# Attention followed by a squared-ReLU MLP: the order in which the MLP visits blocks of tokens and parts of the inner dimension

## The chip, the core and the metric

The kernel runs on one core of a Trainium2 chip. The metric is the time of one execution on the device in microseconds (us), lower is better. Engines go by the profile's names: PE (TensorE), DVE (VectorE), ACT (ScalarE), POOL (GpSimd) and SP (SyncE, which issues the transfers here).

## What is computed

Four batches of 576 tokens go through attention with 8 heads of 64 and a learned position bias; the result, 2304 tokens by 512, goes through an MLP with an inner dimension of 2048. Everything comes and leaves in float32.

```python
def _attn_ref(q, k, v, w1, b1, w2):                 # (4, 8, 576, 64)
    scores = scale * np.matmul(q, k.transpose(0, 1, 3, 2)) + bias(w1, b1, w2)
    attn = softmax(scores)
    return np.matmul(attn, v)

def _moe_ref(x, w_in, w_out):                       # x 2304 x 512, d_ff 2048
    h = x @ w_in
    r = np.maximum(h, 0.0)
    g = r * r
    return g @ w_out
```

## The kernel before

The attention fills the first 373 us and is not touched, but for two small copies that the change adds near its end. The rest, from 373 us to the end, is the MLP, and this text is about it.

**Blocks and parts.** The tokens are cut into five blocks: blocks 0 to 3 are the first 512 tokens of each batch (256 columns wide, since a block is worked on as two halves by a seven-product scheme that saves an eighth of the matmuls), and block 4, `B` in the code and "the tail" in this text, is the 64 last tokens of all four batches, 128 columns wide. The inner dimension is cut into eight parts `P` of 256. One **item** is a block with a part, (n, P); there are 40 of them, and the list `items` gives their order. Items are numbered by their place in that list, from 0.

**One item.** `up(i)` makes 42 matmuls on PE into two PSUM tiles, `ha` (24) and `hb` (18). ACT (line 758) and DVE (lines 760 to 763) put the products together from PSUM; then comes the squared ReLU, on ACT for items below `GA` (lines 765 and 766) and on DVE from there on (line 768). ACT then rounds the result to `gh` (line 773) and DVE takes the remainder `gl` (line 774). `down(i)` makes 24 matmuls (12 for the tail) on four PSUM tiles `y0` to `y3` (two for the tail). The loop emits `up(i)` and then `down(i - 1)`. `ha`, `hb` and each `y` have one buffer, so `up(i + 1)` needs the ACT and DVE readers of item i to be done, and the first `down` of a visit needs the tiles `y` of the visit before it to have been read.

**Visits.** A run of items of one block is a visit. `y` is summed in PSUM over a visit. If a block has another visit to come, its four tiles `y` are copied to tiles `o` and stored to HBM (`py`, line 812). When it comes back, `o` is loaded from there (line 801), DVE adds `y` to it (line 802), and the sum goes out (line 814). Before the change each of the blocks 0 to 3 has two visits of four items, and the tail one of eight, in the middle. The tiles `o` share one ring of two buffers, `stage`, with the loads of raw weights.

**Conversions.** Weights are brought as 64-bit words and are converted on the chip. 24 conversions are left when the MLP starts. `convert(k)` after `up(i)` emits k of them, by the table `WC`; the list `todo` has their order. A conversion of a `w_out` piece is ACT (lines 177 and 243), DVE (lines 180 to 183) and POOL (line 244). One of a `w_in` piece has lines 177 and 180 to 183 too, then POOL (lines 235 to 237), ACT (line 224) and DVE (line 225).

**Splits.** Before the first item of a block its inputs are scaled and split into high and low halves: `split_x`, on POOL (line 626), ACT (line 628) and DVE (line 629), seven pieces (fourteen half-size ones for the tail). It is emitted two items ahead of the block. The scale comes from two one-column matmuls on PE behind an `hb` (line 195). The split inputs of blocks 0 to 3 go to HBM (`store_x`) and are loaded again for the later visit (`load_x`).

A scheduler moves instructions within these rules, so that the order on each engine is not that of the code.

Of the kernel before, what the change touches and what calls it, by code (L numbers as in the profile page):

```python
# [21 lines left out]
B, H, S, D = 4, 8, 576, 64  # L22
# [13 lines left out]
WB, WS, LW, XS, XB, LAG, NE, SC, SN, AH = 40, 3, 4, 48, 70, 1, 13, 22, 16, 2  # L36
WC = (2, 2, 2, 1, 1, 1, 1, 2, 1, 2, 1, 2, 1, 1, 1)
MD, K0, E2, BW, KP, PN, KA = 0x15555, 2, 1, 1, 2, 1, 1
C0, ND, NG, GA, QA, WU, QS = 2, 2, 4, 18, 12, 32, 2
BO, B1 = (3, 5, 8, 10, 13, 15, 18, 20), (12, 3, 8)  # L40
# [9 lines left out]
SC = 41  # L50
SN = 12
AH = 2
WC = (2, 2, 2, 0) + (1,) * 16
ND = 3
NG = 4
GA = 18
KA = 4
QA = 0
WU = 12
# [19 lines left out]
def attention_then_relu2_mlp(ctx: ExitStack, tc: tile.TileContext, q, k, v, cols, w_in, w_out, psi, xmat, dist, out):  # L79
    nc = tc.nc  # L80
    PE, DVE, ACT, POOL, SP = nc.tensor, nc.vector, nc.scalar, nc.gpsimd, nc.sync
# [12 lines left out]
    xT = [keep.tile([128, HP, S], F32, name=f"xT{b}") for b in range(AB)]  # L94
# [67 lines left out]
    def column(w=1):  # L162
        used[0] += w
        return small[:, used[0] - w:used[0]]
# [20 lines left out]
    def largest(src, col):  # L185
        return DVE.tensor_reduce(out=col, in_=src, axis=AX.X if len(src.shape) == 2 else AX.XY, op=ALU.max, apply_absolute_value=True)
# [60 lines left out]
    def is_in(n):  # L247
        return n // 2 % 2 == 0
# [12 lines left out]
    def x_pieces(n):  # L261

        if n < B:
            return [(slice(0, 256), xT[n][:, :, 0:256], xT[n][:, :, 256:512])]
        return [(slice(64 * r, 64 * r + 64), xT[r][:, :, 512:], xT[2 + r][:, :, 512:]) for r in range(2)]

    def x_largest(n):
        cols = column(HP)
        if n < B:
            for c in range(HP):  # L270
                largest(xT[n][:, c, 0:512], cols[:, c:c + 1])
        else:
            for b in range(B):
                largest(xT[b][:, :, 512:], cols[:, b:b + 1])
        return cols


# [269 lines left out]
    todo = [(ic, jb) for ic in chunks for jb in range(0, NJB, 2 if ic == TAIL else 1)]  # L547
# [42 lines left out]
    NB, NP = B + 1, NF // 2  # L590
# [13 lines left out]
    def operand(t):  # L604
        t = t.bitcast(F16).rearrange("p (x c t) -> p x c t", x=2, c=2)
        return t[:, 0], t[:, 1]
# [7 lines left out]
    def split_x(n):  # L614
        sig, w = xsig[n], width[n]
        for m in ORDER:
            hi, lo = (x[:, :, :w] for x in split_to[n % 2][m])
            one, op, two = RIGHT[m]
            if m in XA:
                t = take(0, 9856, 512).rearrange("p (c t) -> p c t", c=2)  # L620
            elif op:
                t = stage_p["p"].tile([128, 2, 256], F32, name="xs", tag="wa", bufs=2)
            for cs, *half in x_pieces(n):
                src = half[one[1]][:, 2 * one[0]:2 * one[0] + 2]
                if op:
                    POOL.tensor_tensor(out=t[:, :, cs], in0=src, in1=half[two[1]][:, 2 * two[0]:2 * two[0] + 2], op=op)
                    src = t[:, :, cs]
                ACT.activation(out=hi[:, :, cs], in_=src, func=AF.Identity, scale=sig)
                DVE.scalar_tensor_tensor(out=lo[:, :, cs], in0=src, scalar=sig, in1=hi[:, :, cs], op0=ALU.mult, op1=ALU.subtract)  # L629
            xs_t[n, m] = (hi, lo)  # L630

    def store_x(n):
        xs_dram[n] = dram.tile([128, 7 * 512], F32, name=f"xs{n}")
        SP.dma_start(out=xs_dram[n], in_=xs_at[n % 2])

    def load_x(n):
        if n % 2 == 0:
            places = [(xs_at[0], range(1, 8))]
        else:
            places = [(xT[2].rearrange("p c s -> p (c s)"), range(1, 5)), (xT[3].rearrange("p c s -> p (c s)"), range(5, 8))]  # L640
        for t, ms in places:
            SP.dma_start(out=t[:, :512 * len(ms)], in_=xs_dram[n][:, 512 * (ms[0] - 1):512 * ms[-1]])
            for k, m in enumerate(ms):
                xs_t[n, m] = operand(t[:, 512 * k:512 * k + 512])
# [8 lines left out]
    for s in range(NU + TL + 1):  # L653
# [32 lines left out]
        if s == XS:  # L686
            pw = ps.tile([128, 512], F32, name="pw", tag="aux", bufs=4)
            set_scale(0, x_largest(0), pw[:, 0:1])
        if s == XB:
            split_x(0)  # L690
        if s < AB * HP * TAIL:
            n, r = divmod(s, AB * HP)
# [7 lines left out]
        if 0 <= s - TL - 1 < NU:  # L700
            values(s - TL - 1)
            b, hp, ic = units[s - TL - 1]
# [17 lines left out]
    ph_p = ctx.enter_context(tc.tile_pool(name="ph", bufs=1, space=PSUM, reuse_waits="tile"))  # L720
    py_p = ctx.enter_context(tc.tile_pool(name="py", bufs=1, space=PSUM, reuse_waits="tile"))

    runs = [(n, 0, NP // 2) for n in range(B)] + [(B, 0, NP)] + [(n, NP // 2, NP) for n in reversed(range(B))]
    items = [(n, P) for n, p0, p1 in runs for P in range(p0, p1)]
    firsts = {(n, p0) for n, p0, p1 in runs}
    lasts = {(n, p1 - 1) for n, p0, p1 in runs}
    part_y = {}
# [3 lines left out]
    def up(i):  # L731
# [31 lines left out]
        stt(out=c[:, 2:4], in0=hb[:, 1:3, :w], scalar=alpha, in1=c[:, 2:4], op0=ALU.mult, op1=ALU.add)  # L763
        if i < GA:
            ACT.activation(out=c, in_=c, func=AF.Relu)
# [58 lines left out]
    def chain_x(n, cols):  # L824
        def run(ps_col):
            set_scale(n, cols, ps_col)
        chains.append(run)


    todo = [4 * P + 2 + f for P in range(NP // 2) for f in range(2)]  # L830
    for P in range(NP // 2, NP, 2):
        todo += sorted(range(4 * P, 4 * P + 8), key=lambda n: (is_in(n) == (P > NP // 2), n))
    done = loaded = 0
    def convert(k):
        nonlocal done, loaded
        for _ in range(k):
            while loaded < min(len(todo), done + AH):
                load_w(todo[loaded])
                loaded += 1
            if done < len(todo):  # L840
                n = todo[done]
                (split_in if is_in(n) else split_out)(n, wdst[n])
                done += 1
# [4 lines left out]
    for i in range(len(items) + LAG):  # L848
        if i == NP // 2:
            tmp_stack.close()  # L850
            late = ctx.enter_context(tc.tile_pool(name="late", bufs=1, side="right", reuse_waits="tile"))
            for n in (4 * NP - 2, 4 * NP - 1):
                t = late.tile([128, 2, 512], F32R, name=f"w{n}")
                wdst[n] = (t[:, 0], t[:, 1])
        if i < len(items):
            n, P = items[i]
            up(i)
            if i + 2 < len(items) and items[i + 2] in firsts and items[i + 2][1] == 0:
                split_x(items[i + 2][0])
            if P == 0 and n < B:  # L860
                store_x(n)
            if P == NP // 2 and n:
                load_x(n - 1)
            if i + 4 < len(items) and items[i + 4] in firsts and items[i + 4][0] not in alpha_t:
                xcols = x_largest(items[i + 4][0])
            if i + 3 < len(items) and items[i + 3] in firsts and items[i + 3][0] not in alpha_t:
                chain_x(items[i + 3][0], xcols)
        convert(WC[i] if i < len(WC) else 0)
        if i >= LAG:
            down(i - LAG)  # L870
# [50 lines left out]
```

## Time and profile before

| | before |
|---|---|
| median of 3 runs | 770.84 us (769.87 to 771.76) |
| the profiled execution: its own time | 769.29 us |
| its span in the trace | 767.2 us |
| busy: PE, DVE, ACT, POOL | 720.3, 570.4, 437.0, 178.8 us |
| mean granted clock of PE, as a share of 2.4 GHz | 0.971 |
| moved by DMA | 71.13 MB, 93 GB/s over the span |

The profiled execution is one of many, and its trace is what all rows below come from. Its own time is 2.1 us longer than its span, and 1.55 us below the median. A matmul's end is modelled, so PE counts as busy where it is merely supplied; what can be read well is where PE sat idle and what ended the wait.

### The profile page before, as it was taken

To read this page: it belongs to the slowest core of one execution; us is meant where nothing else is said; L and a number is where in the kernel's file an instruction comes from. 1 tells how busy PE (TensorE), PEld (TensorE's weight loads), DVE (VectorE), ACT (ScalarE), POOL (GpSimd) and SP (SyncE) were. 2 spreads that over 40 slices of the span, in tenths; PEclk is the share of its full clock that TensorE was granted. 3 is DMA by queue.
4 is the path that set the end of the run, shared out by engine and by line. 5 is a ranking of instruction groups with operands and counts; after the bars stand their busy time and mean duration, and the time that the engine had idled before them with its cause. 6 is when DMAs were issued, how large, how long until landed. Compare 5 with 4: busy or idle time off the path is not lost.

```text
span 767.2 us, 18165 instructions
## 1 busy us (share of the span) xinstructions
PE 720.3 (94%) x7382; PEld 575.6 (75%) x7382; DVE 570.4 (74%) x1184; ACT 437.0 (57%) x900; POOL 178.8 (23%) x281
## 2 busy tenths in 40 slices
PE   6999999999989999898888989989999999999994
PEld 6867778777767777666677867878778888888883
DVE  6689888865767678888789797696988656565553
ACT  4467787877646688977566665655643322222220
POOL 1464323231301032432335234141321000000000
PEclk7599999999989999999999999999999999999998
DMA  7520000000485522232123213134331233230202
GB/s 214 170 91 18 18 2 3 2 2 19 124 289 193 184 81 70 72 125 96 51 75 152 110 56 151 56 156 147 110 111 62 69 118 110 86 108 15 83 28 82
DMA packets 32887, 71.13 MB, mean 93 GB/s; under 512 B 5796, under 2 KB 13988, under 8 KB 31780
## 3 DMA queue, kind: packets, MB, share of 16 engines
q1 hardware_dynamic: 32804, 69.98, 26.9%
q8 instruction: 58, 0.95, 0.5%
q14 instruction: 25, 0.20, 0.1%
HBM read 53.71 MB, written 16.25 MB: 91 GB/s over the span
## 4 chain that ended last, share of the span: by engine, by line
PE 66%; DVE 16%; ACT 7%; issue 4%; DMA 4%; POOL 3%; SPq 0%; DVEq 0%; POOLq 0%; ACTq 0%
PE y L793 19%; PE ha L744 9%; PE px L507 9%; PE sp L433 9%; PE pp L489 7%; PE hb L744 6%; PE bb L381 4%; PE bb L400 2%; DVE area L629 2%; ACT p L444 2%; DMA stage<-in_w_in 2%; DVE mask L370 1%; DVE gl L774 1%; DVE wa L182 1%; DVE t L439 1%
## 5 line engine op out<-in xcount | busy, mean ns | idle before, releaser
L793 PE MATMUL y<-w,gh 128*128 128x512 f32 x576 | 173.1, 401 | 7.5 <-ACT gh L773 7.3
L744 PEld LDWEIGHTS <-area 128*128 128x128 f16 x1680 | 146.6, 98 | 37.5 <-issue 11.3
L793 PEld LDWEIGHTS y<-w,gh 128*128 128x128 f32 x576 | 105.9, 190 | 29.7 <-ACT gh L773 8.9
L439 DVE CUSTOM_DVE_ANT_0 t<-sp,area 128x576 f32<-128x576 f32 x144 | 103.8, 751 | 29.1 <-PE sp L433 26.2
L444 ACT ACTIVATE p<-t,negm 128x576 f32<-128x576 f32 x144 | 111.0, 773 | 25.2 <-DVE negm L439 25.0
L433 PE MATMUL sp<-k,q 64*128 64x288 f32 (+1 forms) x640 | 103.2, 433 | 9.8 <-DVE negm L439 5.3
L793 PE MATMUL y<-w,gl 128*128 128x512 f32 x288 | 103.1, 395 | 0.0
L490 ACT COPY pt<-pp 128x512 f32<-128x512 f32 x144 | 79.9, 583 | 35.3 <-PE pp L489 35.1
L507 PE MATMUL px<-pt,v 128*64 128x128 f32 (+1 forms) x1600 | 97.9, 269 | 2.0 <-DVE bt L387 1.2
L507 PEld LDWEIGHTS px<-pt,v 128*64 128x64 f32 x1600 | 80.1, 137 | 19.0 <-issue 6.7
L744 PE MATMUL ha<-area 128*128 128x256 f16 (+1 forms) x768 | 81.1, 260 | 5.7 <-DVE area L761 2.4
L489 PE MATMUL pp<-ident,p 128*128 128x128 f32 x576 | 84.5, 283 | 1.7 <-ACT p L444 1.3
L433 PEld LDWEIGHTS sp<-k,q 64*128 64x128 f32 (+1 forms) x640 | 53.9, 177 | 31.7 <-issue 11.6
L489 PEld LDWEIGHTS pp<-ident,p 128*128 128x128 f32 x576 | 62.2, 142 | 20.5 <-issue 9.5
L392 POOL TENSOR_TENSOR area<-bt,bt 128x256 f32<-128x256 f32 x72 | 54.1, 776 | 73.3 <-DVE bt L387 73.3
L370 DVE TENSOR_TENSOR mask<-sdist,theta 128x1024 f16<-128x1024 f16 x81 | 56.0, 728 | 13.3 <-PE bb L400 7.2
L744 PE MATMUL hb<-area 128*128 128x256 f16 (+1 forms) x576 | 60.9, 259 | 1.1 <-DVE area L763 0.9
L793 PEld LDWEIGHTS y<-w,gl 128*128 128x128 f32 x288 | 53.1, 188 | 11.2 <-DVE gl L774 0.4
L773 ACT CAST gh<-area 128x512 fp32r<-128x512 f32 (+1 forms) x40 | 22.3, 574 | 60.3 <-DVE area L768 42.1
L774 DVE TENSOR_TENSOR gl<-area,gh 128x512 fp32r<-128x512 f32 (+1 forms) x40 | 28.4, 720 | 24.3 <-ACT gh L773 21.8
L773 ACT CAST gh<-xT 128x512 fp32r<-128x512 f32 (+1 forms) x36 | 19.7, 570 | 40.1 <-PE y L793 22.2
L381 PEld LDWEIGHTS <-mask 128*128 128x128 f16 x1152 | 37.4, 100 | 4.9 <-issue 3.7
(155 smaller groups left out, 1003.4 us busy)
## 6 DMA issues: line engine op xcount, KB each, us to landing
stage<-in_w_in SPq DMA_DIRECT2D x32, 512.0 KB, 3.7
stage<-in_w_out SPq DMA_DIRECT2D x16, 512.0 KB, 3.5
xs<-area SPq DMA_DIRECT2D x4, 1792.0 KB, 5.8
v<-in_v SPq DMA_DIRECT2D x16, 320.0 KB, 4.0
out<-o SPq DMA_DIRECT2D x18, 256.0 KB, 2.0
q<-in_q SPq DMA_DIRECT2D x32, 128.0 KB, 3.0
py<-o SPq DMA_DIRECT2D x16, 256.0 KB, 2.0
o<-py SPq DMA_DIRECT2D x16, 256.0 KB, 2.6
```

The costliest lines, as they stand in the source:

```text
L370: DVE.tensor_tensor(out=out, in0=win, in1=th, op=ALU.is_ge)
L381: PE.matmul(bb[:, 64 * (7 - r):64 * (8 - r)], lhsT=m[:, r], rhs=wmov[:, n], start=(n == 0), stop=(n == 1))
L392: POOL.tensor_tensor(out=dst, in0=tw, in1=sw, op=ALU.add)
L433: mm = PE.matmul(out_t[to, x, :HALF], lhsT=qt[rows, cols], rhs=kt[rows, k0:k0 + HALF], start=True, stop=True)
L439: DVE.tensor_tensor_reduce(out=t.rearrange("p (x n) -> p x n", x=2), in0=sp[:, :, :HALF], in1=bias.rearrange("p (x n) -> p x n", x=2), sca ...
L444: ACT.activation(out=p[:, S * n:S * n + S], in_=t, func=AF.Exp, bias=negm[:, n:n + 1], scale=-1.0, accum_out=sums[:, 2 * ic + n:2 * ic + n ...
L489: PE.transpose(pp[:, 128 * c:128 * c + 128], p[:, k0:k0 + 128], ident)
L490: ACT.copy(pt[:, 4 * h:4 * h + 4], pp.rearrange("p (c m) -> p c m", c=4))
L507: PE.matmul(px[64 * h:64 * h + 64, :w], lhsT=vt[:, c, h], rhs=src, start=(c == 0), stop=(c == 4))
L744: PE.matmul(h[:, s, :w], lhsT=a, rhs=x, start=(k == 0), stop=(k == 5))
L773: ACT.copy(gh, g)
L793: PE.matmul(y, lhsT=a[:, slot, o:o + 128], rhs=x, start=((n, P) in firsts and f == 0 and m == 0), stop=((n, P) in lasts and f == 1 and m = ...
```

## The change

The order of visits becomes a staircase. Blocks 0 to 2 have parts 0 to 3, block 3 parts 0 to 5; then back: block 2 and block 1 with parts 4 and 5, block 0 with parts 4 to 7; then forth: blocks 1, 2 and 3 with parts 6 and 7; the tail comes last, with all eight parts. Blocks 1 and 2 so have three visits, blocks 0 and 3 two, and the tail one. In items: 0 to 15 are the same but for 12 to 17, which are now one visit of block 3; 18 and 19 are block 2, 20 and 21 block 1, 22 to 25 block 0, 26 and 27 block 1, 28 and 29 block 2, 30 and 31 block 3, and 32 to 39 the tail (before: 16 to 23).

The 24 conversions now come in the plain order of parts, and `WC` spreads them out to item 25 (before: to item 19), with none at items 6, 10 and 14 to 17. `GA` goes from 18 to 26. The tail columns of blocks 2 and 3 are copied by ACT into a free part of `xT[0]` (`keep_tails`), because their own place is overwritten by a reload before the tail is split. Split inputs are reloaded by visit and not by block.

```diff
-WC = (2, 2, 2, 0) + (1,) * 16
+WC = (2, 2, 2, 0, 1, 1, 0, 1, 1, 1, 0, 1, 1, 1, 0, 0, 0, 0, 1, 1, 1, 1, 1, 1, 1, 1)
-GA = 18
+GA = 26
-        return [(slice(64 * r, 64 * r + 64), xT[r][:, :, 512:], xT[2 + r][:, :, 512:]) for r in range(2)]
+        return [(slice(64 * r, 64 * r + 64), xT[r][:, :, 512:], tail_x(2 + r)) for r in range(2)]
+
+    def tail_x(b):
+        return xT[0][:, :, 64 * (b - 2):64 * (b - 2) + 64]
+
+    def keep_tails():
+        for b in range(2, B):
+            ACT.copy(tail_x(b), xT[b][:, :, 512:])
-    runs = [(n, 0, NP // 2) for n in range(B)] + [(B, 0, NP)] + [(n, NP // 2, NP) for n in reversed(range(B))]
+    runs = [(0, 0, 4), (1, 0, 4), (2, 0, 4), (3, 0, 6), (2, 4, 6), (1, 4, 6), (0, 4, 8), (1, 6, 8), (2, 6, 8), (3, 6, 8), (B, 0, 8)]
+    run_of = {(n, p0): r for r, (n, p0, p1) in enumerate(runs)}
-    todo = [4 * P + 2 + f for P in range(NP // 2) for f in range(2)]
-    for P in range(NP // 2, NP, 2):
-        todo += sorted(range(4 * P, 4 * P + 8), key=lambda n: (is_in(n) == (P > NP // 2), n))
+    todo = [4 * P + 2 + f for P in range(NP // 2) for f in range(2)] + list(range(4 * (NP // 2), 4 * NP))
-            if P == NP // 2 and n:
-                load_x(n - 1)
+            r = run_of.get((n, P))
+            if r == 3:
+                keep_tails()
+            if r is not None and r + 1 < len(runs) - 1 and runs[r + 1][1] and r + 1 not in (4, 7):
+                load_x(runs[r + 1][0])
```

**What moves, first place: DVE around item 8, where block 2 begins and its split has just run.** The names are `wa` and `zw` (weights in conversion, out and in), `ha` and `hb` with the products of items 7 and 8, `xT1` and `area` (the scratch that item's sums are put together in). Before, DVE has here:

```order
L225 SCALAR_TENSOR_TENSOR area_79<-zw_7380,small_84,area_79 128x896
L763 SCALAR_TENSOR_TENSOR area_79<-hb_7320,small_84,area_79 128x512
L180 TENSOR_SCALAR wa_7591<-wa_7591 128x512
L760 SCALAR_TENSOR_TENSOR xT1_77<-ha_7415,small_84,xT1_77 128x2x256
L761 SCALAR_TENSOR_TENSOR xT1_77<-ha_7415,small_84,xT1_77 128x2x256
```

and now (the lines 760, 761 and 763 are 768, 769 and 771 in the changed file):

```order
L771 SCALAR_TENSOR_TENSOR area_79<-hb_7307,small_84,area_79 128x512
L183 SCALAR_TENSOR_TENSOR wa_7466<-stage_7365,wa_7466 128x512
L180 TENSOR_SCALAR zw_7575<-zw_7575 128x512
L181 TENSOR_SCALAR zw_7575<-zw_7575 128x512
L182 SCALAR_TENSOR_TENSOR zw_7575<-stage_7464,zw_7575 128x512
L183 SCALAR_TENSOR_TENSOR zw_7575<-stage_7464,zw_7575 128x512
L768 SCALAR_TENSOR_TENSOR xT1_77<-ha_7399,small_84,xT1_77 128x2x256
L769 SCALAR_TENSOR_TENSOR xT1_77<-ha_7399,small_84,xT1_77 128x2x256
```

The long last step of a `w_in` conversion has gone from ahead of item 7's last sum; the four first steps of another one have come between item 7's last sum and item 8's first two. The stretch now has the same pattern as the one around item 4, where nothing changes.

**Second place: DVE and PE at the end of a visit that comes back.** `o` is the stored partial sum, `y0` to `y3` the PSUM tiles, `gl` the remainder. Before, at the end of block 3's second visit (items 24 to 27, a visit of four), DVE has:

```order
L802 TENSOR_TENSOR o_9334<-o_9334,y0_9067 128x512
L802 TENSOR_TENSOR o_9341<-o_9341,y1_9068 128x512
L774 TENSOR_TENSOR gl_9310<-xT1_77,gh_9309 128x512
L774 TENSOR_TENSOR gl_9314<-xT1_77,gh_9313 128x512
L802 TENSOR_TENSOR o_9348<-o_9348,y2_9069 128x512
L802 TENSOR_TENSOR o_9355<-o_9355,y3_9070 128x512
```

and now, at the end of block 2's new second visit (items 18 and 19, a visit of two, with a conversion under way):

```order
L182 SCALAR_TENSOR_TENSOR wa_8752<-stage_8637,wa_8752 128x512
L810 TENSOR_TENSOR o_8662<-o_8662,y0_8549 128x512
L183 SCALAR_TENSOR_TENSOR wa_8752<-stage_8637,wa_8752 128x512
L782 TENSOR_TENSOR gl_8629<-xT1_77,gh_8628 128x512
L782 TENSOR_TENSOR gl_8633<-xT1_77,gh_8632 128x512
L810 TENSOR_TENSOR o_8670<-o_8670,y1_8550 128x512
L810 TENSOR_TENSOR o_8678<-o_8678,y2_8551 128x512
L768 SCALAR_TENSOR_TENSOR area_79<-ha_8691,small_84,area_79 128x512
L769 SCALAR_TENSOR_TENSOR area_79<-ha_8691,small_84,area_79 128x512
L770 SCALAR_TENSOR_TENSOR area_79<-hb_8692,small_84,area_79 128x512
L771 SCALAR_TENSOR_TENSOR area_79<-hb_8692,small_84,area_79 128x512
L810 TENSOR_TENSOR o_8686<-o_8686,y3_8552 128x512
```

The second partial sum can be loaded only when line 183 has read the raw weights out of the same ring, and the fourth add now stands behind the sums of item 21. PE, which before went through all 24 products of the next visit's first `down` in one piece, now has in that `down`, of item 20:

```order
L801 MATMUL y2_8762<-w18_6530,gh_8628 128x512 x2
L801 MATMUL y2_8762<-w18_6530,gl_8629 128x512
L801 MATMUL y1_8761<-w19_6531,gh_8632 128x512 x2
L801 MATMUL y1_8761<-w19_6531,gl_8633 128x512
L801 MATMUL y2_8762<-w19_6531,gh_8632 128x512 x2
L801 MATMUL y2_8762<-w19_6531,gl_8633 128x512
L752 LDWEIGHTS area_79
L752 MATMUL ha_8788<-area_79 128x256
```

The 18 products on `y0`, `y1` and `y2` are followed by 14 products `ha` of item 22, and only then come the six on `y3`. The visit of items 20 and 21 ends in the same way.

**Third place: SP at the end of the program.** `o` and `py` are the partial sums, `out` the result. Before:

```order
L801 DMA o_10312<-py0_7072 128x512
L801 DMA o_10322<-py1_7079 128x512
L814 DMA out_0<-o_10312 128x512
L814 DMA out_0<-o_10322 128x512
L801 DMA o_10332<-py2_7086 128x512
L801 DMA o_10342<-py3_7093 128x512
L814 DMA out_0<-o_10332 128x512
L814 DMA out_0<-o_10342 128x512
L917 UNCONDITIONAL_BRANCH
```

and now:

```order
L809 DMA o_9881<-py2_8468 128x512
L809 DMA o_9888<-py3_8475 128x512
L822 DMA out_0<-o_9881 128x512
L822 DMA out_0<-o_9888 128x512
L825 DMA out_0<-o_10390 2x64x512
L825 DMA out_0<-o_10400 2x64x512
L926 UNCONDITIONAL_BRANCH
```

The program ended with a visit that loads partial sums in two rounds; it ends now with the tail's two stores, which load nothing.

In numbers: partial sums are stored and loaded 24 times each (before: 16), so there are 8 more stores, loads and adds; the final visit has eight half-size items; two ACT copies are added; everything else is the same work in another order.

## Rows read from the trace of the kernel before

**Rows 1.** First line of the page.

```profile
span 767.2 us, 18165 instructions
```

**Rows 2.** Busy time in four stretches: us, then PE, PEld, DVE, ACT, POOL, PEclk, DMA, GB/s.

```profile
402.80:509.10 106.30, 99.03 (x641) 80.28 (x640) 91.01 (x136) 66.93 (x91) 37.37 (x32) 0.98 0.31 120
509.10:600.60 91.50, 88.91 (x723) 73.19 (x724) 74.05 (x141) 47.58 (x83) 19.59 (x24) 1.00 0.29 100
600.60:757.00 156.40, 156.40 (x1014) 131.32 (x1014) 91.91 (x122) 37.03 (x49) 0.00 (x0) 1.00 0.21 71
757.00:767.20 10.20, 0.46 (x3) 0.04 (x1) 2.48 (x4) 0.00 (x0) 0.00 (x0) 0.69 0.44 154
```

**Rows 3.** PE in order of time: start, duration, instruction, count, idle before and releaser.

```profile
509.11 2.11 PE L793 MATMUL y<-w,gh 128*128 128x512 f32 x8 [1.92 <-ACT gh L773]
...
577.26 1.51 PE L744 MATMUL ha<-area 128*128 128x128 f16 x24
...
582.44 1.51 PE L744 MATMUL ha<-area 128*128 128x128 f16 x24
...
640.91 2.79 PE L744 MATMUL ha<-area 128*128 128x256 f16 x24
...
645.42 0.70 PE L793 MATMUL y<-w,gh 128*128 128x512 f32 x2
...
651.00 2.79 PE L744 MATMUL ha<-area 128*128 128x256 f16 x24
```

**Rows 4.** The chain that ended last, its last 30 us: start, duration, what.

```profile
746.53 10.26 PE y L793 x45
...
756.82 0.70 DVE o L802
...
757.54 2.02 DMA out<-o
...
759.62 2.72 DMA o<-py
...
763.34 0.69 DVE o L802
```

**Rows 5.** Groups by line and form, 430 to 768 us: count, busy, mean ns, idle before.

```profile
L804 DVE COPY o<-y 128x256 f32<-128x256 f32 x2 | 0.8, 422 | 0.1
L805 ACT COPY o<-y 128x256 f32<-128x256 f32 x2 | 0.7, 369 | 3.4 <-DVE o L804 3.4
L225 DVE SCALAR_TENSOR_TENSOR area<-zw,small,area 128x896 f16<-128x896 f32 x7 | 9.1, 1294 | 1.1 <-ACT area L224 1.1
L183 DVE SCALAR_TENSOR_TENSOR wa<-stage,wa 128x512 uint32<-128x512 uint32 x8 | 6.4, 800 | 0.1
```

**Rows 6.** PE around item 8, from item 6's scale matmuls to item 7's first y.

```profile
440.59 0.28 PE L195 MATMUL hb<-small,ones 128*128 128x1 f32 x2
...
468.27 2.09 PE L793 MATMUL y<-w,gh 128*128 128x512 f32 x8
```

**Rows 7.** PE and DVE around item 4: item 2's scale matmuls, item 4's second sum.

```profile
397.06 0.28 PE L195 MATMUL hb<-small,ones 128*128 128x1 f32 x2
...
420.40 0.73 DVE L761 SCALAR_TENSOR_TENSOR xT<-ha,small,xT 128x512 f32<-128x512 f32 x1
```

**Rows 8.** Three short stretches at two waits of PE, columns as in group 2.

```profile
451.00:453.50 2.50, 0.06 (x1) 0.00 (x0) 2.46 (x6) 2.50 (x5) 0.00 (x0) 1.00 0.00 0
453.50:457.20 3.70, 3.66 (x9) 2.49 (x10) 3.70 (x6) 1.23 (x2) 2.80 (x4) 0.54 0.08 23
416.00:423.00 7.00, 4.67 (x34) 3.61 (x32) 6.93 (x10) 5.19 (x7) 4.76 (x6) 1.00 0.55 207
```

**Rows 9.** DVE's adds at the end of items 24 to 27; then all transfers of `o`.

```profile
639.07 1.37 DVE L802 TENSOR_TENSOR o<-o,y 128x512 f32<-128x512 f32 x2
...
644.53 1.46 DVE L802 TENSOR_TENSOR o<-o,y 128x512 f32<-128x512 f32 x2 [2.25 <-DMA o<-py]
...
DMA to landing us min/median/max: 2.0/2.3/4.9
```

## What the change will do to the time

> **What bounds the kernel now.** I read the page first, for the span of 767.2 us [rows 1], and then the busy times of the MLP in four stretches, to see where PE is not fed [rows 2]. From 600.6 to 757 us, when no conversion and no split is left, PE is busy for all of 156.4 us: there only PE's own work counts. Ahead of that, from 402.8 to 600.6 us, PE sits idle for 7.3 and 2.6 us, while DVE is at 86 and 81 per cent. Behind it, in the last 10.2 us, PE works for 0.46 us. So there are three places to gain or lose: the stretch of the first blocks, the stretch with the tail, and the end. PE in order of time gives the measure [rows 3]: a full item takes 651.00 - 640.91 = 10.09 us, of which `up` is 645.42 - 640.91 = 4.51 and `down` 5.58; a half-size item takes 582.44 - 577.26 = 5.18 us. None of this PE work is changed by the change; its order is. The sum below is what the waits around it become.
>
> **The end of the program: -5.4 us.** The chain that ended last shows it [rows 4]. PE is through with 45 of the last 48 products at 746.53 + 10.26 = 756.79 us and, with the 0.46 us of [rows 2], ends at 757.46. Then the ring of two buffers runs a second round: an add, a store of 2.02 us, a load of 2.72 us, two more adds, the last of them over at 763.34 + 0.69 = 764.03, and a last store up to 767.2. That is 9.7 us after PE's end. With the tail last, nothing is loaded. DVE copies half of the last `y` in 0.42 us, ACT the other half in 0.37 (the trace has ACT behind DVE there) [rows 5], and the last store takes what it took before, 767.2 - 764.03 = 3.2 us. With 0.3 us for hand-overs that is 4.3 us; 9.7 - 4.3 = 5.4 us less. The bounds are 4.9 and 5.9: a hand-over more or less.
>
> **The tail out of the middle: -4.1 us.** From the first product of `down(11)` at 509.11 [rows 3] to the start of `up(25)` at the end of the second stretch of [rows 2], 600.6 us, PE has five `down` and four `up` of full size and eight half-size items: 4 x 10.09 + 5.58 + 8 x 5.18 = 87.4 us. It took 91.5, so 4.1 us are lost there, in the conversions, the tail's split and half-size items that leave each other too little time. In the changed order the items that follow 11 are full ones, and 14 to 17 carry no conversion at all; this is the regime of the third stretch of [rows 2], where PE never waits. What hides the later conversions (items 18 to 25) is PE's 10.09 us per item. DVE had 91.91 us in the 15.5 items of the third stretch, 5.9 per item. A conversion is four passes of at most 0.80 us, and 1.29 more for a `w_in` piece [rows 5], so at most 3.2 or 4.5 us, and the second add per visit-end item is 0.7 more: 9.8 to 11.1 us at the very most. `GA` takes the squared ReLU off DVE in these items, so that I take them as covered. If that cover were gone, it would cost up to 1 us in each of the four items with a `w_in` piece: bounds 0 and -4.1 for this part as a whole.
>
> **The first blocks: -0.5 us.** Here the change does less than its table says. Around item 4 nothing moves. Around item 12 the same conversions stay between the same rows of DVE, since the scheduler had pulled them up already, so the wait of 1.92 us before `down(11)` [rows 3] stays. Around item 8 one conversion is put in the place of another. From item 6's scale matmuls to item 7's first product with `y` PE took 468.27 - 440.59 = 27.7 us [rows 6]; its work in there is two `down`, two `up` and some 2.4 us of `ha` and scale matmuls, 22.6 us, so that 5.1 us are lost. In the changed order the pattern on DVE is that of item 4, where item 4's second sum was over at 420.40 + 0.73, 24.1 us behind the scale matmuls at 397.06 [rows 7]. PE has item 9's `ha` next, for 2.2 us, which needs just that sum; so `down(7)` starts after 26.3 us and not 27.7, and PE waits some 3.6 us in one piece for it. That gain of 1.4 us is uncertain, for what the wait does to the clock: after a wait of 2.5 us at 451 the granted clock was 0.54 for 3.7 us, near the lower level of 1.2 GHz, which lost 3.7 x 0.46 = 1.7 us, while around one of 2.3 us between 416 and 423 (7.00 - 4.67) it remained at 1.00 [rows 8]. I take an even chance of such a fall: 1.4 - 0.85 = 0.5. Bounds: a gain of 5.1, if no wait is left, and a loss of 1.8, if the fall comes and the new conversion's weights land 1.5 us late, which they may because their load now stands on SP behind the early reload of block 1's split inputs into `xT[2]`.
>
> **The ends of visits: +0.7 us.** Stored sums make eight more round trips, all behind PE unless they hold back a `y`. At the end of a visit of four, DVE's second pair of adds was over at 644.53 + 1.46 = 645.99 [rows 9], and `y2` was first needed two products of `y` behind 645.42, 1.4 us later, at 646.8 [rows 3]: hidden, with 0.8 us to spare. At the two new visit ends with conversions (items 19 and 21) I take T as the end of the visit's last `down`. Line 183 frees the second buffer at about T - 0.6; a load of 2.7, an add of 0.7, a store of 2.0 [rows 4], a load and an add put `y3` free at T + 8.2. PE needs it after `up` (4.5), 18 of 24 products (4.2) and 14 of `ha` (1.5): at T + 10.2. With 2.0 us to spare I count 0.7 in all for six ends, between 0 and the price of the third rival.
>
> **The tail at the end: +1.2 us.** Its split, fourteen pieces on ACT and DVE with four adds among them, is emitted with item 30 and has one `down`, one `up` and most of a second `down` (14.3 us) before PE asks for it. I count 0.7 us; the bounds are 0 and the 4.1 us that the tail cost with conversions. The last half-size item has only the `down` before it, 2.8 us, as cover for eight steps of about 0.42 us (the half copy of [rows 5] is the nearest row), 3.4 us: 0.5 us of wait; bounds 0 and 1. The two ACT copies fall at the end of the attention, into ACT's waits for DVE, and cost nothing there; uncovered they would be two copies of half a tile, 0.37 us each [rows 5].
>
> **Sum.** -5.4 - 4.1 - 0.5 + 0.7 + 1.2 = -8.1 us, against the profiled execution's own 769.29: 761.2. The median of the runs is 1.55 us above that execution, so I forecast 762.7 us for the median.
>
> **Rivals.** (1) *The waits of the first blocks vanish*, because PE no longer meets a conversion at item 8: 4.6 us more come back, 758.1. For it speaks that the table has no conversion at items 6 and 10; against it that the order still puts one there. (2) *Only the end pays.* The late conversions fill DVE to its 10.09 us and the tail's 4.1 us come back as waits in items 18 to 31: 766.8. For it speaks the upper bound of 11.1 us, against it that PE never waited where DVE had 5.9. (3) *The ring becomes the bound, and the kernel is slower.* Transfers of `o` took between 2.0 and 4.9 us [rows 9], and in the new visits weights and reloads share the queue. With 4.9 for each, the chain at items 19 and 21 ends at T + 15.5, 5.3 us late, and at the other four ends, where the first add is over at T - 1.4 (`y0` is done three quarters of a half `down` ahead of T), a store, a load and an add put `y2` free at T + 9.1; it is needed at T + 5.9, so 3.2 late: 2 x 5.3 + 4 x 3.2 = 23 us, and 1.7 for each fall of the clock. That is 785 us without the falls; it decides as soon as the six ends lose 1.9 us each on average, 11.2 us in all instead of the 0.7 in the sum, which puts the time above 773.2. Against it speaks the median of 2.3. The Trainium skill ("TensorE: Matmul & The Clock Gate", section "HAM oscillation — how this bites in real kernels") says that short bursts of products between waits for transfers can bring the clock down again at every burst; by that rule each of the six ends with a wait of its own would pay the 1.7 us too, 10 us in all. The trace agrees with it at one wait of 2.5 us and not at one of 2.3. (4) *No change to speak of*: (2) with half of (3), about 771.
>
> **How the numbers follow.** About 0.3% (2.3 us) is what a measurement of this kernel can tell from no change. I give my forecast (760 to 765) 0.50, (1) 0.14, (2) 0.18, (4) 0.07 and (3) 0.11. Faster by more than 0.3%, under 768.5, are the first three: 0.82; within it 0.07; slower 0.11. For 8 times in 10 the range takes the forecast, nearly all of (1) and most of (2): 756.8 to 768.5.
>
> **What would show it.** PE's end to the span's end should be 4 to 5 us, with no load in the last chain. Items 13 to 17 should stand 10.1 us apart. A wait of 1.9 us should remain before `down(11)`, and one of 3 to 4 us before item 9's `ha`, released by line 769. At the ends of items 19 and 21 the first product on `y3` should not wait. The forecast is wrong if PE waits for the adds of line 810 at several visit ends, if the granted clock falls more than twice in the MLP, or if item 32 starts more than 2 us late.

## The result: slower, and the profile after

The changed kernel takes 775.15 us in the median of 10 runs (772.38 to 776.98), the kernel before, timed beside it, 771.3. The ratio is 1.0051, with a 95% interval of 1.0029 to 1.0073. The forecast was 762.7. The profiled execution took 776.84 us, its first page line is

```profile
span 775.0 us, 18223 instructions
```

which is 7.8 us more than in [rows 1]. Where it went is read from three stretches, cut by what PE does and not by the clock as [rows 2] are: from the MLP's first product to `down(11)`, from there to PE's end, and the rest. The kernel before (us, PE, PEld, DVE, ACT and POOL busy, granted clock, DMA share, GB/s):

```profile
373.62:509.11 135.49, 124.58 (x817) 101.15 (x816) 116.73 (x180) 84.78 (x115) 48.17 (x40) 0.99 0.29 110
509.11:757.46 248.35, 245.77 (x1736) 204.54 (x1736) 166.40 (x263) 84.60 (x131) 19.59 (x24) 1.00 0.24 82
757.46:767.20 9.74, 0.00 (x1) 0.00 (x0) 2.02 (x4) 0.00 (x0) 0.00 (x0) 0.68 0.46 162
```

The changed kernel:

```profile
374.96:512.71 137.75, 126.09 (x816) 102.56 (x815) 115.87 (x176) 84.56 (x115) 45.62 (x40) 0.98 0.31 115
512.71:760.13 247.42, 246.88 (x1736) 205.74 (x1736) 162.75 (x268) 102.71 (x146) 19.45 (x24) 0.99 0.29 100
760.13:775.00 14.87, 0.00 (x1) 0.00 (x0) 0.57 (x2) 0.70 (x2) 0.00 (x0) 0.59 0.10 35
```

The end of the program, which was to shrink by 5.4 us, grew by 14.87 - 9.74 = 5.1. The first part of the MLP grew by 2.3, the second shrank by 0.9; the MLP started 1.3 later, which is scatter (in the five executions of the two kernels that were profiled it started between 373.6 and 376.9). 5.1 + 2.3 - 0.9 + 1.3 = 7.8. The two profiled executions stand 1.7 us above and 2.0 us below the medians of the ten runs, so that the medians differ by 3.9 us only, where these two differ by 776.84 - 769.29 = 7.5; the growth of the end is not part of that scatter (experiment 9 has it again).

**What the end waits for.** The last copies on ACT in the changed kernel, in order of time:

```profile
760.40 0.70 ACT L813 COPY o<-y 128x256 f32<-128x256 f32 x2 [3.07 <-DVE o L812]
```

SP's last issues:

```profile
760.80 1.29 SPq L825 DMA_DIRECT2D out<-o  x2
```

And slices of 3 us from there (columns as above):

```profile
763.00:766.00 3.00, 0.00 (x0) 0.00 (x0) 0.00 (x0) 0.00 (x0) 0.00 (x0) 0.50 0.13 38
766.00:769.00 3.00, 0.00 (x0) 0.00 (x0) 0.00 (x0) 0.00 (x0) 0.00 (x0) 0.50 0.13 51
769.00:772.00 3.00, 0.00 (x0) 0.00 (x0) 0.00 (x0) 0.00 (x0) 0.00 (x0) 0.50 0.13 51
772.00:775.00 3.00, 0.00 (x0) 0.00 (x0) 0.00 (x0) 0.00 (x0) 0.00 (x0) 0.50 0.07 27
```

The copies are over at 761.1, as forecast. SP issues the two stores of the tail by 762.1, and then no engine works. The DMA share is 0.13, that is 2 of 16 engines, at 51 GB/s, for some 12 us: two tiles of 256 KB. The sign was there in the kernel before, in a stretch where PE was never idle, so that nothing drew the eye to it. This is the first of the same two stores, in the middle, where SP issued it at 600.94 and the second only at 609.21:

```profile
603.00:606.00 3.00, 3.00 (x26) 2.65 (x24) 2.13 (x5) 1.25 (x2) 0.00 (x0) 1.00 0.13 39
606.00:609.00 3.00, 3.00 (x15) 2.47 (x14) 2.59 (x3) 0.23 (x1) 0.00 (x0) 1.00 0.13 46
```

The tail's rows lie in two batches, so its store has the pattern 2x64x512, with an outermost size of 2. The Trainium skill says why this matters ("DMA: Bandwidth & Descriptors", section "Why a DMA increments its semaphore by 16 and not by 1"): the number of engines is the largest one up to 16 that divides the slowest dimension, larger than 1, of both patterns. By that rule 2x64x512 gets two engines; the share of 0.13 agrees.

**PE's waits in the changed kernel**, from PE's instructions in order of time:

```profile
421.60 3.67 PE L801 MATMUL y<-w,gh 128*128 128x512 f32 x8 [2.33 <-ACT gh L781]
...
468.16 3.32 PE L752 MATMUL ha<-area 128*128 128x256 f16 x20 [3.48 <-DVE xT L769]
...
512.71 2.93 PE L801 MATMUL y<-w,gh 128*128 128x512 f32 x8 [1.90 <-ACT gh L781]
...
632.12 0.73 PE L801 MATMUL y<-w,gh 128*128 128x512 f32 x2 [0.52 <-DVE o L810]
```

Behind each of the first three the clock fell. In 5 us from there (columns as above; the third last is the granted clock):

```profile
421.00:426.00 5.00, 4.40 (x17) 3.29 (x18) 5.00 (x7) 2.10 (x4) 3.53 (x4) 0.66 0.04 16
468.90:473.90 5.00, 5.00 (x24) 3.73 (x23) 3.88 (x4) 2.97 (x3) 1.01 (x1) 0.66 0.01 3
512.70:517.70 5.00, 4.99 (x21) 3.56 (x22) 3.42 (x6) 2.00 (x3) 0.00 (x0) 0.66 0.01 3
```

Each fall loses an estimated 5.00 x 0.34 = 1.7 us. The kernel before had one of the same size (453.00 to 458.00 at 0.66) and went through its waits of 2.33 and 1.92 us without any.

### The profile page after: what moved, and what is told of

It is laid out like the page before. It is cut to its first block, busy times and chain, and to the rows that moved or that the text cites. A ratio compares the mean times of both kernels' runs of the same rounds, so it can differ in the third digit from the quotient of the medians.

```text
span 775.0 us, 18223 instructions
## 1 busy us (share of the span) xinstructions
PE 720.9 (93%) x7382; PEld 576.7 (74%) x7382; DVE 564.6 (73%) x1184; ACT 455.5 (59%) x918; POOL 175.6 (23%) x281
## 4 chain that ended last, share of the span: by engine, by line
PE 66%; DVE 15%; ACT 6%; issue 4%; DMA 4%; POOL 3%; DVEq 0%; SPq 0%; ACTq 0%; POOLq 0%
PE y L801 20%; PE ha L752 9%; PE px L514 9%; PE sp L440 8%; PE pp L496 6%; PE hb L752 6%; PE bb L388 4%; DVE area L636 2%; PE bb L407 2%; DMA stage<-in_w_in 2%; ACT p L451 2%; DVE mask L377 1%; DVE t L446 1%; DVE wa L182 1%; PE pa L499 1%
## 5 line engine op out<-in xcount | busy, mean ns | idle before, releaser
L801 PE MATMUL y<-w,gh 128*128 128x512 f32 x576 | 178.3, 404 | 4.8 <-ACT gh L781 4.2
L801 PE MATMUL y<-w,gl 128*128 128x512 f32 x288 | 106.1, 393 | 0.0
L752 PE MATMUL ha<-area 128*128 128x256 f16 (+1 forms) x816 | 88.1, 264 | 7.8 <-DVE xT L769 3.5
L752 PE MATMUL hb<-area 128*128 128x256 f16 (+1 forms) x612 | 64.9, 260 | 0.3 <-DVE area L771 0.2
L633 POOL TENSOR_TENSOR area<-xT 128x512 f32<-128x512 f32 (+1 forms) x16 | 21.2, 1325 | 104.8 <-DVE area L636 104.8
L235 POOL TENSOR_TENSOR zw<-zw 128x256 f32<-128x256 f32 x16 | 12.8, 803 | 140.8 <-DVE zw L183 95.8
L782 DVE TENSOR_TENSOR gl<-xT,gh 128x512 fp32r<-128x512 f32 (+1 forms) x36 | 26.5, 757 | 23.0 <-ACT gh L781 16.2
L388 PE MATMUL bb<-wmov,mask 128*128 128x64 f16 x1152 | 40.7, 196 | 0.4 <-DVE bt L394 0.3
```

The lines of the kernel that those rows point to most:

```text
L388: PE.matmul(bb[:, 64 * (7 - r):64 * (8 - r)], lhsT=m[:, r], rhs=wmov[:, n], start=(n == 0), stop=(n == 1))
L752: PE.matmul(h[:, s, :w], lhsT=a, rhs=x, start=(k == 0), stop=(k == 5))
L782: DVE.tensor_tensor(out=gl, in0=g, in1=gh.bitcast(F32), op=ALU.subtract)
L801: PE.matmul(y, lhsT=a[:, slot, o:o + 128], rhs=x, start=((n, P) in firsts and f == 0 and m == 0), stop=((n, P) in lasts and f == 1 and m = ...
```

## The experiments

Theory A: the tail's store is slow by its pattern, and the change moved it from a place where PE hid it to the end, where all wait for it. Rival B: the end of the program, or memory, is slow whatever the pattern. A second question was where the rest of the missing gain went: the waits and clock falls of the first blocks. "PE part" in what follows is from the MLP's first product to PE's end, "drain" from there to the span's end. Before: 383.8 and 9.7; after: 385.2 and 14.9.

**1. Only the pattern undone.** In the changed kernel:

```diff
-                tails = out.rearrange("(b s) m -> b s m", s=S)[2 * k:2 * k + 2, 512:]
-                SP.dma_start(out=tails, in_=o)
+                for r in range(2):
+                    SP.dma_start(out=out[S * (2 * k + r) + 512:S * (2 * k + r) + S], in_=o[64 * r:64 * r + 64])
```

> The changed kernel, with only its two tail stores written another way: each tile of 128 rows goes out as two stores of 64 rows of 512, instead of one store whose outermost size is 2. Theory A (the store ties itself to 2 of the 16 DMA engines, and takes some 13 us where a store of 128 rows took 2.0): PE's end to the span's end falls from 15.0 us to 4 to 5 us, the DMA share in the last stretch is no longer 0.13, and the median falls by 10 to 11 us, from 775 to about 765, 0.992 of the kernel before. Rival B (the time behind PE's end is the end of the program, or memory that answers late, whatever the pattern): the drain stays at 13 to 15 us and the time at about 775. What is left against the forecast of 762.7 under theory A is 2 to 3 us in the middle, from waits and clock falls there.

Measured: 769.35 us, ratio to before 0.9946 (0.9926 to 0.9965), so 1.05% or 8 us below the changed kernel by the two ratios (0.9946 against 1.0051), less than the 10 to 11 us that A said. PE part 384.8, drain 5.8 us. The last two slices:

```profile
760.00:763.00 3.00, 0.00 (x0) 0.00 (x0) 0.44 (x2) 0.70 (x2) 0.00 (x0) 0.94 0.38 86
763.00:766.00 3.00, 0.00 (x0) 0.00 (x0) 0.00 (x0) 0.00 (x0) 0.00 (x0) 0.50 0.39 89
```

SP's last issues:

```profile
760.54 2.46 SPq L825 DMA_DIRECT2D out<-o  x4
```

Theory A holds: PE's part is unchanged within 0.4 us, and the drain fell by 9.1. It is 1 us longer than A said: four issues of 0.61 us stand in a row on SP, so that the last store starts 1.9 us behind the first (experiment 8 tries this).

**2. The same in the kernel before**, where the stores are in the middle (the same diff).

> The kernel before, with only its two tail stores (in the middle of the MLP, behind item 23) written as two stores of 64 rows each. Theory A: the stretch from 600.9 to 613 us no longer shows a DMA share of 0.13 for some 12 us, but PE was busy there all the time, so that the median stays within 0.3% of the kernel before (771). Rival C (the slow store also held back o's buffers or the weights queued behind it in the middle, so that the pattern has always cost something): 2 us or more faster, under 769.

Measured: 771.43, ratio 0.9985 (0.9967 to 1.0004). The stretch of 603 to 609 us now has

```profile
603.00:606.00 3.00, 3.00 (x30) 2.69 (x29) 2.39 (x4) 1.93 (x5) 0.00 (x0) 1.00 0.38 87
606.00:609.00 3.00, 3.00 (x22) 2.56 (x20) 2.30 (x4) 0.63 (x1) 0.00 (x0) 1.00 0.64 175
```

and PE is as busy as it was. The interval alone would leave room for 2.5 us, but PE's part is 383.7 us against 383.8: the slow store cost nothing that can be measured there, and rival C falls.

**3. A slow pattern at the end of the kernel before, first try.**

```diff
+                rows = out[S * n + 128 * k:S * n + 128 * k + 128]
+                SP.dma_start(out=rows.rearrange("(b s) m -> b s m", b=2) if n == 0 and k > 1 else rows, in_=o)
```

> The kernel before, with only the last two result stores (block 0, rows 256 to 383 and 384 to 511, each 128 rows of 512) written with an outermost size of 2, as the tail's stores are; nothing else moves. Theory A: the last store takes 12 to 14 us instead of 3.2 up to the span's end, at a DMA share of 0.13, so the drain goes from 9.7 to about 20 us and the median from 771 to about 781 (1.013 of the kernel before). Rival B (the pattern does not matter, the tail's rows in memory or the order of the program do): unchanged within 0.3%.

Measured: 772.03, ratio 0.9986 (0.9965 to 1.0006), drain 9.6. That looked like B, but the last store's share was not that of two engines:

```profile
765.00:768.00 3.00, 0.00 (x0) 0.00 (x0) 1.31 (x2) 0.00 (x0) 0.00 (x0) 0.50 0.47 175
```

The two halves lie next to each other in memory, and the built program holds the pattern as 128x512. SP's issues say so too, 0.34 us each, as for the other stores of 128x512, where the tail's take 0.53 and 0.66. The run says nothing on A.

**4. The same with halves that lie apart.**

```diff
+                if n == 0 and k > 1:
+                    rows = out[256:512].rearrange("(b q s) m -> q b s m", b=2, q=2)[k - 2]
```

> The kernel before, with only the last two result stores (block 0, the tiles of rows 256 to 383 and 384 to 511) sent to rows whose two halves do not lie next to each other (rows 256 to 319 with 384 to 447, and 320 to 383 with 448 to 511), so that the pattern's outermost size is really 2; in the run before this one the two halves lay next to each other, and the store stayed fast. In the output rows 320 to 383 and 384 to 447 of block 0 change places. Theory A (an outermost size of 2 is served by 2 of 16 DMA engines; the changed kernel's two tail stores, 512 KB together, took some 13 us at 38 to 51 GB/s): the same two engines carry both stores, PE's end to the span's end goes from 9.7 to 18 to 20 us, DMA share 0.13 there, the median from about 772 to about 781, 1.012. Rival B (the pattern does not matter): unchanged within 0.3%.

Measured: 783.79, ratio 1.0142 (1.011 to 1.0174); drain 19.6 us. SP's last issues:

```profile
767.87 1.50 SPq L817 DMA_DIRECT2D out<-o  x2
```

Three slices behind them:

```profile
771.00:774.00 3.00, 0.00 (x0) 0.00 (x0) 0.00 (x0) 0.00 (x0) 0.00 (x0) 0.50 0.13 45
774.00:777.00 3.00, 0.00 (x0) 0.00 (x0) 0.00 (x0) 0.00 (x0) 0.00 (x0) 0.50 0.13 52
777.00:780.00 3.00, 0.00 (x0) 0.00 (x0) 0.00 (x0) 0.00 (x0) 0.00 (x0) 0.50 0.13 51
```

The pattern alone, in the old order, costs 19.6 - 9.7 = 9.9 us of drain. B is refuted. (The median rose by 11.9; PE's part is 385.8 in this profile, 2 us more than before, with a second fall of the clock.)

**5. The conversions out of the first blocks.** Experiment 1 with

```diff
-WC = (2, 2, 2, 0, 1, 1, 0, 1, 1, 1, 0, 1, 1, 1, 0, 0, 0, 0, 1, 1, 1, 1, 1, 1, 1, 1)
+WC = (2, 2, 2, 0, 1, 1, 0, 0, 0, 1, 0, 0, 0, 1, 1, 1, 1, 1, 1, 1, 1, 1, 1, 1, 1, 1)
```

> The changed kernel with the stores of 64 rows, and besides with other entries in WC (2,2,2,0,1,1,0,0,0,1,0,0,0,1,1,...): no conversion in items 7, 8, 10, 11 and 12, so that none stands on DVE ahead of the split products of items 8 and 12, and the conversions come one per item from 13 on. Theory A': the waits ahead of item 9's ha (3.48 us, for line 769) and ahead of item 11's down (1.90 us, for line 781) are the conversions' doing; both go, and the clock falls that came behind each (1.5 to 1.7 us lost for each) with them: 5 to 8 us less than the other kernel with stores of 64 rows, 757 to 760. Rival D (the waits come from the splitting of the block itself, or come back at a later item since 13 conversions now follow each other): within 2 us of that kernel, 763 to 767.

Measured: 758.84, ratio 0.9814 (0.9784 to 0.9844). PE part 376.7 (374.7 in experiment 8, where the clock did not fall), drain 5.8. The list of PE's waits from 404 us to its end (line, what it waited for, us, times, longest):

```profile
PE y L801 <- ACT gh L781: 2.3, 1, 2.3
PE y L801 <- DVE gl L782: 0.9, 1, 0.9
PE y L801 <- DVE o L810: 0.5, 1, 0.5
```

The waits of 3.48 and 1.90 us are gone with the conversions, and nothing took their place later on. PE's part is 8.1 us shorter than in experiment 1: 4.7 us of waits (8.4 there by the same list, 3.7 here), and the rest mostly the clock, which fell twice in experiment 1, once for 7.1 us at 0.55, and once here. D falls. The medians differ by 10.5 us, 2.5 more than A' allowed; the intervals are wide enough for that.

**6. The same items freed in the old order**: the kernel before with

```diff
-WC = (2, 2, 2, 0) + (1,) * 16
+WC = (2, 2, 2, 0, 1, 1, 0, 0, 0, 1, 0, 0, 0, 2, 2, 2, 2, 2, 2, 2, 1)
```

> The kernel before, in its old order, with conversions moved out of items 6 to 8 and 10 to 12 as in the fastest kernel so far: WC is 2,2,2,0,1,1,0,0,0,1,0,0,0 and then two for each item from 13 to 19 and one in item 20, since the old order needs all of them by item 23. Theory E (the late conversions can be paid for only by the new order, in which items 13 to 25 are full items of 10.09 us on PE; here they fall on the tail's half-size items of 5.18 us): the waits before down(7) and down(11), 2.5 and 1.9 us, go, but 4 us or more of new waits come up between items 16 and 23, and the kernel stays within 0.5% of before (768 to 776). Rival F (the table alone does it, whatever the order): 4 to 7 us faster, 765 to 768.

Measured: 787.87, ratio 1.0201 (1.0176 to 1.0225). In the tail's items PE stands idle for 52.00 - 38.38 = 13.6 us, and the clock falls three times; the slice that holds them:

```profile
561.00:613.00 52.00, 38.38 (x304) 31.56 (x305) 37.98 (x70) 17.11 (x30) 11.28 (x15) 0.90 0.22 72
```

In the kernel before, PE idled for 91.50 - 88.91 = 2.6 us from 509.10 to 600.60, the tail's items included [rows 2]. F falls, and E's place was right, but its price was far too low. Of the two waits that were to go, the one before `down(11)` went; the one of 2.47 us, which stands before `down(6)`, became 1.34. Late conversions need room to hide under, and the old order has the tail's half-size items there. But the table also has two conversions in each of the items 13 to 18, where the new order had one; how much of the 13.6 us is due to the half-size items and how much to the pairs is not shown, nor was a table tried that spreads them out to item 23.

**7. Block 1's split freed too.** Experiment 5 with WC starting 3,3,0,0,0,0, and 2,2 at items 13 and 14.

> The fastest kernel so far (changed order, stores of 64 rows, late conversions) with the early conversions moved up as well: WC starts 3,3,0,0,0,0 instead of 2,2,2,0,1,1, so that block 1's split (around item 4) has none beside it, and 2,2,1,1,1,... from item 13. Theory A': the wait of 2.33 us before down(3) (released by line 781) goes, and with it a fall of the clock in some runs: 2 to 4 us less than that kernel, 755 to 757 at 772 for the kernel before, 0.979. Rival G (three conversions each in items 0 and 1 hold back PE there, where it had 2.4 us of wait already): the same time or up to 3 us more, 759 to 762.

Measured: 764.85, ratio 0.9905 (0.988 to 0.9929), 7 us worse than experiment 5 by the ratios. The wait before `down(3)` did not go; it moved ahead, before `down(2)`, and grew. PE in order of time:

```profile
412.99 3.78 PE L801 MATMUL y<-w,gh 128*128 128x512 f32 x8 [3.67 <-ACT gh L781]
```

The clock around that wait, half speed for nearly all of 11 us:

```profile
411.00:422.00 11.00, 8.37 (x19) 6.15 (x20) 10.35 (x11) 4.36 (x7) 7.09 (x5) 0.53 0.00 0
```

Block 1's split on DVE (line 636) began at 408.03, behind a conversion of a `w_in` piece:

```profile
407.42 0.69 DVE L183 SCALAR_TENSOR_TENSOR zw<-stage,zw 128x512 uint32<-128x512 uint32 x1
408.03 0.74 DVE L636 SCALAR_TENSOR_TENSOR area<-xT,small,area 128x512 f16<-128x512 f32 x1
```

In experiment 5 it began at 403.30:

```profile
403.30 0.75 DVE L636 SCALAR_TENSOR_TENSOR area<-xT,small,area 128x512 f16<-128x512 f32 x1 [1.43 <-ACT area L635]
```

The pairs of conversions at items 13 and 14 cost something as well, 1.7 us in two waits, before `down(14)` and `down(15)`, that experiment 5 does not have:

```profile
541.24 2.11 PE L801 MATMUL y<-w,gh 128*128 128x512 f32 x8 [1.31 <-ACT gh L781]
...
551.98 2.11 PE L801 MATMUL y<-w,gh 128*128 128x512 f32 x8 [0.40 <-ACT gh L781]
```

Worse, as G said, but by more and at other places than G named.

**8. The tail's halves on two queues.** Experiment 5 with `(SP, ACT)[r].dma_start` for the two halves.

> The fastest kernel so far (changed order, stores of 64 rows, late conversions), with the second half of each of the two tail tiles stored from ACT's queue instead of SP's. Theory H (what is left at the end is four issues of 0.61 us each on one engine, 2.45 us, and then the last store): PE's end to the span's end falls from 5.8 to about 4.6 us. Rival I (the last store's own time counts, or the issue on ACT is slower): 5.5 us or more. Either is too small for the median to tell surely: 758 plus or minus 1.5.

Measured: 757.76, ratio 0.9818 (0.9794 to 0.9842); drain 5.3, between H and I. ACT's two issues took 0.72 us each, SP's 0.59, and from issue to landing the four stores took 2.4 to 3.1 us, where experiment 1 had 2.3 to 2.4. This version and that of experiment 5 are equal within their intervals, and both beat both kernels.

**9. The changed kernel twice more, and the kernel before once more, for the clock.**

> The changed kernel again, unaltered, for one more profiled execution. In its first one the clock fell three times in the MLP, behind waits of 2.33, 3.48 and 1.90 us. Theory J (the waits belong to the kernel, the falls are decided anew in each execution): the three waits stand again within 0.1 us, but one or more of the three falls are missing here or in the second repeat, and the spans differ by about 1.7 us for each. Rival K (the kernel decides): the same three falls again.

> As the run before: the same kernel, one more execution. Theory J: the same waits, another set of falls. Rival K: the same three falls.

> The kernel before again, unaltered. In its first profile the clock fell once in the MLP, behind the wait of 2.47 us, and not behind those of 2.33 and 1.92 us. Theory J: the same waits within 0.1 us (but for that of 2.47 us, which was 1.1 to 1.3 us wherever the one of 2.33 us brought a fall), any of them with a fall or without. Rival K: one fall, behind the wait of 2.47 us.

Measured, one execution each: 779.0, 778.65 and 770.76 us. The changed kernel had the same three waits and the same three falls both times, as K said; PE part 386.6 and 385.1, drain 14.9 and 14.8 (9.6 in the kernel before). The kernel before had its one fall at another place than in its first profile, as J said. PE in this repeat:

```profile
421.73 3.60 PE L793 MATMUL y<-w,gh 128*128 128x512 f32 x8 [2.33 <-ACT gh L773]
455.24 2.14 PE L793 MATMUL y<-w,gh 128*128 128x512 f32 x8 [1.24 <-ACT gh L773]
```

The clock there:

```profile
421.00:426.00 5.00, 4.28 (x16) 3.24 (x17) 5.00 (x7) 2.23 (x4) 3.54 (x4) 0.66 0.10 42
```

But experiment 1, the same kernel up to its last stores, went through the wait of 2.33 us at full clock, against K:

```profile
421.90:426.90 5.00, 5.00 (x31) 4.09 (x32) 5.00 (x7) 1.70 (x3) 3.13 (x4) 1.00 0.01 2
```

And the wait before `down(11)`, 1.89 to 1.92 us in all nine executions that have it at that length, brought a fall in all four of the new order (three of the changed kernel and experiment 1) and in none of the five of the old one (two of the kernel before and experiments 2 to 4). The kernel before, in its first profile, behind that wait:

```profile
509.10:514.10 5.00, 4.99 (x31) 4.08 (x32) 4.96 (x9) 2.20 (x4) 2.94 (x3) 1.00 0.10 35
```

So the length of a wait alone does not decide a fall, neither theory holds throughout, and what decides it stays open.

## Why the prediction was wrong, step by step

**The end of the program: the step that failed.** The prediction's "the last store takes what it took before, 767.2 - 764.03 = 3.2 us" took the price of a store of 128x512, which ran at a DMA share of 0.47 in experiment 3, for one of 2x64x512 at 0.13. One behind the other, the tail's two stores take some 13 us. The drain became 14.9 us instead of 4.3: 10.6 of the 15.9 us by which the forecast of the span missed (-8.1 against +7.8); in the medians it missed by 775.15 - 762.7 = 12.45. Everything else in that step held: nothing is loaded, and the copies ended 1.0 us behind PE. With the pattern undone, the drain is 5.8 (experiment 1); the 1.5 us left of the miss come with four issues in a row in place of one, and half of them on another queue bring 0.5 us back (experiment 8). The pattern 2x64x512 stood in the rows of SP that were shown for the change, and the prediction priced it by another store's row.

**The first blocks: -0.5 forecast, +2.3 measured.** Both waits stood where they were expected (1.90 us before `down(11)`, and 3.48 before item 9's `ha`, released by line 769). The mechanism was right, two sizes were not. PE and DVE around item 8 in the changed kernel:

```profile
443.46 0.28 PE L195 MATMUL hb<-small,ones 128*128 128x1 f32 x2
...
467.36 0.74 DVE L769 SCALAR_TENSOR_TENSOR xT<-ha,small,xT 128x512 f32<-128x512 f32 x1
...
471.13 2.85 PE L801 MATMUL y<-w,gh 128*128 128x512 f32 x8
```

Item 8's second sum was over 24.6 us behind the scale matmuls, not 24.1, and item 9's `ha` took 3.0 us and not 2.2, with the clock down. So `down(7)` began 471.13 - 443.46 = 27.7 us behind them, as before, and the gain of 1.4 us did not come. And the clock fell behind two waits of this stretch instead of one, and a third time right behind 512.71; the forecast had counted half a fall, at one wait only. More than two falls in the MLP was the prediction's own sign of being wrong.

**The tail out of the middle, the ends of visits, the tail at the end: -4.1 + 0.7 + 1.2 = -2.2 forecast, -0.9 measured, -2.6 without the third fall.** PE was busy for all of 512.71 to 605 us. The visit ends cost one wait of 0.52 us in the whole of the MLP, for `y3` at the end of the visit of items 20 and 21, where the prediction had expected none; the tail's start cost none. The sum came within 0.4 us, without the third fall, but by luck in part: the last two terms cost 0.5 us and not 1.9, so that about 3.1 us and not 4.1 are left as the gain of the middle.

**The rivals.** (1) did not happen by this change, since the order kept a conversion at both splits, but experiment 5 shows that it was to be had. (2) named the wrong half: the end did not pay. (3) was on the right side by luck, for a wrong reason: the transfers of `o` kept their medians of 2.0 us (stores) and 2.6 (loads), though the longest took 6.0 and not 4.9, and PE waited 0.5 us for them. The Trainium skill's rule that was weighed there ("TensorE: Matmul & The Clock Gate", section "HAM oscillation — how this bites in real kernels") was hardly put to the test: PE waited at one end of a visit, for 0.52 us. The falls of this trace came behind waits for ACT and DVE, not for transfers.

## What to carry to other kernels

Before work is moved to the end of a program, price its last transfer by its own pattern, in the place where it now runs hidden: a DMA share of 0.13 under a busy PE costs nothing there and 10 us at the end. An order that looks worse by its first time may be one line from being better: with the stores by rows it is 0.5% faster than before, and with the conversions moved to where the new order has room, 1.9%. A reordering and the table that places the side work belong together: freeing the same items in the old order, with the conversions in pairs behind them, made that kernel 2% slower.

## What the runs showed that was not expected

Two stores with an outermost size of 2, issued one behind the other, shared the same two engines: with both in flight the share stayed at 0.13, so that the two together took as long as one after the other. A pattern whose halves lie next to each other was joined when the program was built, and its store ran at a share of 0.47. The profile's figure from issue to landing did not show any of this, since it has none for the tail's two stores (its median of 2.0 us is that of other stores to `out`); the DMA share by slices did. And a wait of 2.33 us, the same to 0.01 us in twelve profiled executions (both orders, line 773 or 781), brought a clock fall in seven of them and none in five, and both with one and the same kernel, the one before: none in its first profile, one in the repeat.
